# Three tokens of a head side by side on a partition for the first k and q, and the last row tile in two PSUM banks: a sparse attention with a gated FFN on one core

## The chip, the cores and the metric

The kernel runs on one core of a Trainium2 chip (trn2). The metric is the time of one execution on the device in microseconds (us). The engines are called as in the profile: PE (TensorE, matmuls and transposes), PEld (the loading of weights into PE), DVE (VectorE), ACT (ScalarE), POOL (GpSimd) and SP (SyncE, which issues most transfers).

## What is computed

For 4 batches, 8 heads, 768 tokens and 64 values a head, a query may look at the 6 best of the 24 chunks of 32 keys; a bound from each chunk's smallest and largest key decides which. The result, one row of 512 for each of 3072 tokens, goes through a root mean square norm and a gated FFN.

```python
ub = np.sum(np.maximum(q[:, :, :, None, :] * k_min[:, :, None, :, :], q[:, :, :, None, :] * k_max[:, :, None, :, :]), axis=-1)
ub = np.where(causal, ub, -1000000000.0)
top_chunks = np.argsort(ub, axis=-1)[..., -top_k:]
scores = scale * np.matmul(q, k.transpose(0, 1, 3, 2))
...
mask = sel & (pos[:, None] >= pos[None, :])
scores = np.where(mask, scores, -1000000000.0)
...
return np.matmul(attn, v).astype(np.float32)
```

```python
rms = np.sqrt(np.mean(x * x, axis=-1, keepdims=True) + 1e-06)
xn = x / rms * rms_g
g = xn @ w_gate
silu = g * (1.0 / (1.0 + np.exp(-g)))
val = xn @ w_val
return (silu * val @ w_out).astype(np.float32)
```

## The kernel before

**Work.** The 32 heads are taken as 16 pairs, four pairs a batch. For each pair `prep` (L487) loads k and q (tile names `knat`, `qnat`), turns them on PE (`turn`, L522, tiles `pk` and `pq`), copies them out of PSUM to `kt` and `qt` (`out_`, L535), takes each chunk's smallest and largest key, computes the bounds (`ub`, from pair 6 on for two pairs at once in `duo`, L778), turns these back (`up`), and picks the chunks on DVE. `scores` (L851) then does the scores (`sc`, L876), the exponentials on ACT (`pt`, L893) and the product with v (`av`, L912). When all four pairs of a batch are done, `norm` (L945) makes the normed rows and turns them (`tp` on PE for the first batch, a transposing transfer for the others) into `xT`, and `ffn` (L1025) does, for each half batch of 384 rows, 12 gate and 12 value products (`gp` L1045, `vp` L1066) and then three row tiles of 128 rows with 12 projections each (`po`, L1086), a copy out of PSUM (`osb`, `poE`) and an output transfer of 128 x 512 values (L1101).

**Loads of k and q.** `load` (L499) issues one transfer for each head of the pair (four for each tensor of pair 0, which is loaded in two halves of three row tiles). Token t of a head lies on partition t mod 128, so each partition takes one token of 64 f32 values, 256 bytes in a run, six times for each head. In the tile the two heads of a token lie side by side. `turn` transposes, for each of three row tiles, 128 partitions x 128 values (both heads) at once; three such results, 384 tokens in their order, fill one PSUM bank. From pair 3 on (`QM`, `side_q`) the natural q is also copied to `qn` and turned by a transfer; for the first three pairs the turned and cast q is used alone.

**Order.** Every piece of work is a step of a planner (`Order`, L79) with an engine, a duration, what it depends on, and the buffers it opens. `run` (L98) plays the steps through in a plan of its own: whenever an engine is free there, it takes the ready step with the lowest rank whose buffers are free. A step's rank is the sum of its place (`TIMES`: a for a pair's preparation, l for its loads, s for its scores, n and f for norm and FFN, and a pace for each step within these) and of its kind (`RANK`). The steps are then written out in the plan's order, and each engine of the chip works through its own list in that order, waiting where data is not there yet.

**Fillers.** 88 steps called `busy` (L346) multiply zeros: 48 (`BUSY`) of 512 columns (rank 1000, 1001 and so on), ready from the start, and 40 (`LATER`) of 256 columns, ready after the third pair's last scores (L920 to L923). Their ranks are above those of the other PE steps in the first batch, so that the plan puts them where PE has nothing else; all of them are in PE's list somewhere. They keep PE working while it would wait.

Of the kernel before, what the change touches and what calls it, by code (L numbers as in the profile page):

```python
# [8 lines left out]
FP32 = mybir.dt.float32  # L9
# [18 lines left out]
        av=439.71, dif=-349.0, eps=-276.35, exp=56.9, kC=119.11, kE=221.89, kT=-479.5,  # L28
        kload=-91.99, kmn=-561.73, kmx=-221.73, max=-117.69, qC=120.39, qE=644.67, qN=97.14,
        qT=303.27, qX=110.23, qload=17.43, relu=-156.64, root=392.56, sc=392.96, sel=176.91,  # L30
        selC=388.0, selT=-168.59, sq=-325.5, tp=-47.15, tpE=460.17, ub=-387.44, ubE=-1000.64,
        ubm=-238.37, up=-379.03, vload=-360.06, xb=-167.37, xs=293.02,
    ),
    dict(
        av=-243.01, dif=-122.81, eps=-968.41, exp=80.0, gate=-57.45, hh=-33.27, kC=474.21,
        kE=54.78, kT=-28.02, kload=327.35, kmn=571.37, kmx=673.95, mask=-6.85, max=351.72,
        out=-338.93, po=268.25, poE=188.61, qE=-4.14, qN=444.8, qT=271.57, qX=-691.62,
        qload=314.07, relu=202.91, root=-1348.37, sc=-186.72, sel=354.08, sq=285.76, tanh=579.3,
        tg=-259.04, ub=-101.04, ubE=-390.25, ubm=307.49, up=-117.99, val=-52.48, vload=103.56,
        xT=119.23, xb=-299.83, xs=-84.52,  # L40
# [161 lines left out]
def kernel(  # L202
# [11 lines left out]
    nc = tc.nc  # L214
# [17 lines left out]
    HW = NT * P + D  # L232
    NPAIRS = B * NP
# [253 lines left out]
    def prep(c, i0, nb, at, lr):  # L487
# [8 lines left out]
        for w, src in (("k", k), ("q", q)):  # L496
            nat[w], big[w] = Buf("nat"), Buf("qt")

            def load(e, w=w, src=src, r0=0, rn=nb):  # L499
                if nat[w].tile is None:  # L500
                    tile_of(nat[w], [P, NT, 2, D], FP32, w + "nat")
                t = nat[w].tile
                for hl in range(2):
                    eng = nc.scalar if p == 0 and hl else nc.sync
                    eng.dma_start(out=t[:, r0:r0 + rn, hl, :],  # L505
                                  in_=src[b, h0 + hl, (i0 + r0) * P:(i0 + r0 + rn) * P].rearrange(
                                      "(t p) d -> p t d", p=P))

            if p == 0:
                ld = [add(w + "load", "SP", 0.2, -200 + 2 * (w == "q") + r0 / 3,  # L510
                          lambda e, load=load, r0=r0: load(e, r0=r0, rn=3), opens=[nat[w]],
                          load=3 * P * 550) for r0 in range(0, nb, 3)]
            else:
                ld = [add(w + "load", "SP", 1.4, rank(lr, b, w + "load"), load, opens=[nat[w]],
                          load=n * 550)] * 2
# [3 lines left out]
            for j0 in range(0, nb, 3):  # L519
                bank = Buf("ps", "prep")  # L520

                def turn(e, w=w, j0=j0, bank=bank):  # L522
                    t = tile_of(bank, [P, 3 * P], FP32, "p" + w)
                    for j in range(3):
# [4 lines left out]
                tr = add(w + "T", "PE", 0.33, rank(at, b, w + "T", j0, "step"), turn, [ld[j0 // 3], c_id],  # L529
# [495 lines left out]
    def ffn(b, c, at, pace):  # L1025
# [52 lines left out]
        for th in range(3):  # L1078
            po, ob = Buf("ps", "po"), Buf("ob")
            prev = None  # L1080
            for part in range(3):
                def proj(e, th=th, part=part, po=po):
                    if part == 0:
                        tile_of(po, [P, DM], FP32, "po")
                    for ht in range(part * 4, part * 4 + 4):
                        nc.tensor.matmul(po.tile[:], hhs[ht].tile[:, th * P:(th + 1) * P],  # L1086
                                         wo[:, ht, :], start=(ht == 0), stop=(ht == NHT - 1))
# [3 lines left out]
                prev = add("po", "PE", 0.867, place("po"), proj,  # L1091
# [3 lines left out]
            def out_(e, po=po, ob=ob):  # L1095
                t = tile_of(ob, [P, DM], FP32, "osb")
                evict(e, t[:], po.tile[:], 0.5)

            o = add("poE", "", {"ACT": act(512), "DVE": dve(512)}, place("poE"), out_, [prev], opens=[ob], uses=[po])
            r0 = b * S + c * W + th * P  # L1100
            add("out", "SP", 0.55, place("out"), lambda e, r0=r0, ob=ob: nc.sync.dma_start(  # L1101
                out=out[r0:r0 + P, :], in_=ob.tile[:]), [o], uses=[ob])
# [56 lines left out]
```

## Time and profile before

| | |
|---|---|
| median of 3 runs | 315.96 us (315.95 to 316.0) |
| profiled execution | 315.79 us |
| its span, first to last instruction | 314.0 us |
| granted PE clock, mean | 1.000 |
| `pk` transposes, all pairs (L525) | 96 |
| `pq` transposes, all pairs (L525) | 96 |
| fillers (L346) | 88, of them 48 of 512 columns and 40 of 256 |
| projections (L1086) | 288, of 512 columns |
| output transfers (L1101) | 24, 256 KB each, the last issued at 310.9 us |
| DMA packets under 512 B | 106224 of 113301 |

In the profile each line of the chain in order of time has a start, a duration and an engine with its tile and line; "x6" is the number of instructions that it holds. A wait for several things is put down to the one that came last. The ends of matmuls are modelled: in lists of instructions by group a matmul of 128 columns has some 0.27 us, from its start to its last result, while the next one starts far earlier; the durations in the chain are from start to start and are the ones to add up.

### The profile page before, as it was taken

How to read it: one execution, taken by the hardware profiler on the slowest of the kernel's cores; microseconds unless marked ns; L12 is line 12 of the kernel's file. 1: busy time of each engine (PE TensorE's matmuls, PEld its weight loads, DVE VectorE, ACT ScalarE, POOL GpSimd, SP SyncE). 2: the span in 40 equal slices, each digit the busy share in tenths (PEclk: the TensorE clock that was granted, in tenths of full speed). 3: DMA queues.
4: the chain of work that ended last, by engine and by line, in shares of the span. 5: the costliest groups of instructions: out<-in, count | busy, mean ns of one | idle time of the engine just before them, and what ended most of it. 6: DMA issues, size and time to landing. Idle time of an engine off the chain costs nothing.

```text
span 314.0 us, 7640 instructions
## 1 busy us (share of the span) xinstructions
PE 308.6 (98%) x2844; PEld 196.1 (62%) x2844; DVE 230.7 (73%) x654; ACT 194.4 (62%) x420; POOL 100.7 (32%) x157
## 2 busy tenths in 40 slices
PE   7999999999999999999999999999999999999995
PEld 4567877666566775666667565656666645655542
DVE  7699986888988487967986799879464663873530
ACT  5589987863475987478579654344988823333321
POOL 8666534342353564045357300001522220000000
PEclk9999999999999999999999999999999999999999
DMA  8999989989989898979934640002341045001102
GB/s 171 210 190 178 145 108 207 198 114 143 196 86 199 126 179 152 201 164 222 158 79 61 93 102 0 2 2 52 84 94 59 20 118 150 3 0 65 38 22 111
DMA packets 113301, 35.36 MB, mean 113 GB/s; under 512 B 106224, under 2 KB 110064, under 8 KB 113264
## 3 DMA queue, kind: packets, MB, share of 16 engines
q1 hardware_dynamic: 83152, 26.62, 40.9%
q0 software_dynamic: 28512, 7.87, 25.6%
q10 hardware_dynamic: 1600, 0.39, 0.6%
q8 instruction: 22, 0.36, 0.5%
q14 instruction: 15, 0.12, 0.1%
HBM read 28.57 MB, written 6.29 MB: 111 GB/s over the span
## 4 chain that ended last, share of the span: by engine, by line
PE 97%; DMA 1%; ACTq 0%; ACT 0%; issue 0%
PE gp L1045 20%; PE vp L1066 20%; PE po L1086 20%; PE sc L876 12%; PE av L912 7%; PE busy L346 4%; PE pq L525 4%; PE pk L525 3%; PE ub L789 2%; PE ub L731 2%; DMA qnat<-in_q_dram 1%; PE up L811 1%; PE sc L882 1%; PE up L755 1%; PE tp L1011 0%; ACTq L505 0%
## 5 line engine op out<-in xcount | busy, mean ns | idle before, releaser
L893 ACT ACTIVATE pt<-sc 128x512 bf16<-128x512 f32 (+2 forms) x192 | 88.4, 578 | 10.1 <-PE sc L876 5.3
L1052 ACT ACTIVATE sg<-gp 128x384 bf16<-128x384 f32 x96 | 47.7, 500 | 62.7 <-PE gp L1045 60.0
L1066 PE MATMUL vp<-xT,wv 128*128 128x384 bf16 x384 | 77.0, 326 | 0.0
L1045 PE MATMUL gp<-xT,wg 128*128 128x384 bf16 x384 | 76.2, 326 | 0.0
L1086 PE MATMUL po<-wo,hh 128*128 128x512 bf16 x288 | 69.3, 379 | 0.0
L1058 DVE SCALAR_TENSOR_TENSOR tg<-sg,gp 128x384 bf16<-128x384 bf16 x96 | 52.2, 548 | 21.7 <-ACT sg L1052 19.5
L1074 DVE TENSOR_TENSOR hh<-vp,tg 128x384 bf16<-128x384 f32 x96 | 51.8, 551 | 11.1 <-PE vp L1066 7.3
L1045 PEld LDWEIGHTS <-wg 128*128 128x128 bf16 x384 | 36.8, 98 | 24.5 <-issue 1.0
L1066 PEld LDWEIGHTS <-wv 128*128 128x128 bf16 x384 | 36.9, 98 | 24.1
L876 PE MATMUL sc<-qs,ke 128*128 128x128 bf16 (+5 forms) x420 | 51.4, 251 | 0.0
L1086 PEld LDWEIGHTS <-hh 128*128 128x128 bf16 x288 | 27.6, 98 | 27.5
L301 POOL CAST ke<-kt 64x768 bf16<-64x768 f32 x31 | 26.4, 852 | 36.9 <-ACT kt L297 17.0
L876 PEld LDWEIGHTS <-ke 128*128 128x128 bf16 (+1 forms) x420 | 30.3, 97 | 11.3 <-issue 1.6
L899 POOL TENSOR_SCALAR_AFFINE_SELECT pt<-pt 128x512 bf16<-128x512 bf16 (+1 forms) x48 | 24.4, 527 | 37.6 <-ACT pt L893 37.4
L912 PEld LDWEIGHTS <-pt 128*128 128x128 bf16 x672 | 28.8, 98 | 7.7 <-POOL ke L301 0.6
L912 PE MATMUL av<-vx,pt 128*128 128x65 bf16 x672 | 32.6, 193 | 0.0
L299 ACT ACTIVATE osb<-po 128x512 f32<-128x512 f32 x19 | 11.4, 602 | 21.4 <-PE po L1086 21.4
L346 PE MATMUL busy<-zeros 128*128 128x512 bf16 (+1 forms) x88 | 20.1, 349 | 1.3 <-DVE zeros L341 1.3
L933 DVE TENSOR_TENSOR xb<-av,rden 128x384 bf16<-128x384 f32 (+1 forms) x34 | 18.1, 534 | 1.2
L989 DVE SCALAR_TENSOR_TENSOR xs<-xb,ri,gains 128x512 bf16<-128x512 bf16 x24 | 16.9, 746 | 2.7 <-DMA xT<-xs 2.1
L301 POOL CAST qn<-qnat 128x768 bf16<-128x768 f32 x10 | 8.2, 821 | 31.9 <-DMA qs<-qn 30.7
L481 POOL DMA_DIRECT2D vx<-in_v_dram x16 | 16.8, 1052 | 4.0 <-PE av L912 2.6
(87 smaller groups left out, 303.1 us busy)
## 6 DMA issues: line engine op xcount, KB each, us to landing
out_dram<-osb SPq DMA_DIRECT2D x24, 256.0 KB, 2.2
knat<-in_k_dram SPq DMA_DIRECT2D x30, 192.0 KB, 4.3
qnat<-in_q_dram SPq DMA_DIRECT2D x30, 192.0 KB, 4.8
vx<-in_v_dram POOLq DMA_DIRECT2D x16, 192.0 KB, 4.7
wg<-in_moe_w_gate_dram POOLq DMA_DIRECT2D x2, 768.0 KB, 8.6
wv<-in_moe_w_val_dram POOLq DMA_DIRECT2D x2, 768.0 KB, 7.8
wo<-in_moe_w_out_dram POOLq DMA_DIRECT2D x2, 768.0 KB, 9.9
qs<-qn SPq DMA_TRANSPOSE x26, 3.3
```

What stands on the lines that cost most here:

```text
L301: engine[e].tensor_copy(out_, in_)
L346: nc.tensor.matmul(t[:, 0:n], zeros[:, 0:P], zeros[:, 0:n], start=True, stop=True)
L876: nc.tensor.matmul(t[:, x:x + m, :].rearrange("p a b -> p (a b)"), ke[kk, kb * P:(kb + 1) * P], qs[kk, q0 * P:(q0 + m) * P], start=not tri ...
L893: nc.scalar.activation(out=t[:, 0:nn, :], in_=sc.tile[:, 0:nn, :], func=ACT.Exp, scale=SCALE)
L899: nc.gpsimd.affine_select(out=pt.tile[:, 0:nd, :], in_=pt.tile[:, 0:nd, :], compare_op=ALU.is_ge, fill=0.0, base=0, pattern=[[0, nd], [1, ...
L912: nc.tensor.matmul(av.tile[:, qi - i0, :], pt.tile[:, x, :], VX[c.v.slot][:, hl * NT + kb, :], start=(begin and m == 0), stop=(left[0] == ...
L1045: nc.tensor.matmul(t[:], wg[:, g, hs], XT[b].tile[:, g, cols], start=(g == 0), stop=(g == NP - 1))
L1052: nc.scalar.activation(out=t[:], in_=gp.tile[:], func=ACT.Tanh, scale=0.5)
L1058: nc.vector.scalar_tensor_tensor(out=t[:], in0=sg.tile[:], scalar=1.0, in1=gp.tile[:], op0=ALU.add, op1=ALU.mult)
L1066: nc.tensor.matmul(t[:], wv[:, g, hs], XT[b].tile[:, g, cols], start=(g == 0), stop=(g == NP - 1))
L1074: nc.vector.tensor_tensor(out=t[:], in0=vp.tile[:], in1=tg.tile[:], op=ALU.mult)
L1086: nc.tensor.matmul(po.tile[:], hhs[ht].tile[:, th * P:(th + 1) * P], wo[:, ht, :], start=(ht == 0), stop=(ht == NHT - 1))
```

## The change

For the first three pairs (`WIDE`), each partition takes three tokens that follow each other, so that a run in memory is 3 x 64 values, 768 bytes; the tile holds the two heads apart: [128, 2 heads, 2 halves, 3 tokens, 64]. Partition p then holds tokens 3p, 3p+1 and 3p+2 of each half of 384. `turn` transposes each of the three token places by itself and writes the columns to every third word of the bank, so the bank holds the 384 tokens in their order as before. Since the two heads no longer lie side by side, one transpose takes 128 values that end with the second head's token place (its lower 64 result rows are right, the upper 64 are those of something else), and a second one of 64 values overwrites the upper 64 rows with the first head. The planner's costs for these steps follow: 0.66 instead of 0.33 for a turn, 330 instead of 550 for a row of a load.

In the last half batch, the third row tile's projection is made in two parts of 256 columns, each with a PSUM tile, a copy and an output transfer of its own.

All values of the planner's tables `RANK` and `TIMES` are replaced; `BUSY`, `LATER`, the slots and the limits are not. Of the tables only some lines are shown here.

```diff
@@ -25,38 +25,38 @@
 
 RANK = (
     dict(
-        av=439.71, dif=-349.0, eps=-276.35, exp=56.9, kC=119.11, kE=221.89, kT=-479.5,
...
+        av=531.52, dif=-599.99, eps=-382.83, exp=-161.96, kC=439.01, kE=22.86, kT=-498.41,
...
 TIMES = {
...
-    133.0, "a7": 70.59, "a8": 128.02, "a9": 121.26, "f0.0": 33.65, "f0.1": 8.37, "f1.0": -84.59,
-    "f1.1": 458.33, "f2.0": 528.25, "f2.1": 57.29, "f3.0": 75.85, "f3.1": 711.78, "ke": 138.67,
...
-    "n3.1": 574.2, "pace0": -0.69, "pace1": 11.25, "pacef0.0": 0.39, "pacef0.1": 15.72,
-    "pacef1.0": 11.97, "pacef1.1": 14.19, "pacef2.0": 25.48, "pacef2.1": 21.31, "pacef3.0":
-    -30.15, "pacef3.1": 4.73, "pacen": -9.51, "qn0": -62.11, "s0.0": -763.02, "s1.0": -94.31,
...
+    "a7": 109.83, "a8": 49.55, "a9": 39.08, "f0.0": -72.94, "f0.1": -64.96, "f1.0": -71.83,
+    "f1.1": -48.5, "f2.0": -120.42, "f2.1": -73.36, "f3.0": -52.32, "f3.1": -51.07, "ke":
...
+    "n3.1": -636.32, "pace0": 0.45, "pace1": 10.85, "pacef0.0": 3.71, "pacef0.1": 19.42,
+    "pacef1.0": 16.78, "pacef1.1": 6.12, "pacef2.0": 20.36, "pacef2.1": 14.59, "pacef3.0":
+    -41.53, "pacef3.1": 9.68, "pacen": -19.58, "qn0": -12.11, "s0.0": -499.62, "s1.0": 233.49,
...
@@ -230,6 +230,7 @@
     DUO = 6
     KSIDE, QM = 16, 3
     HW = NT * P + D
+    WIDE = dict(k=3, q=3)
     NPAIRS = B * NP
 
     SLOTS = dict(ps=8, nat=7, kb=0, qn=2, vext=4, set=3, ku=4, selq=2, qt=7, ubs=1, ubd=1, small=8, ubm=3,
@@ -496,7 +497,19 @@
         for w, src in (("k", k), ("q", q)):
             nat[w], big[w] = Buf("nat"), Buf("qt")
 
-            def load(e, w=w, src=src, r0=0, rn=nb):
+            wide = p < WIDE[w]
+
+            def load(e, w=w, src=src, r0=0, rn=nb, wide=wide):
+                if wide:
+                    if nat[w].tile is None:
+                        tile_of(nat[w], [P, 2, 2, 3, D], FP32, w + "nat")
+                    t, j, jn = nat[w].tile, r0 // 3, rn // 3
+                    for hl in range(2):
+                        eng = nc.scalar if p == 0 and hl else nc.sync
+                        eng.dma_start(out=t[:, hl, j:j + jn],
+                                      in_=src[b, h0 + hl, r0 * P:(r0 + rn) * P].rearrange(
+                                          "(j p t) d -> p j t d", j=jn, t=3))
+                    return
                 if nat[w].tile is None:
                     tile_of(nat[w], [P, NT, 2, D], FP32, w + "nat")
                 t = nat[w].tile
@@ -509,24 +522,32 @@
             if p == 0:
                 ld = [add(w + "load", "SP", 0.2, -200 + 2 * (w == "q") + r0 / 3,
                           lambda e, load=load, r0=r0: load(e, r0=r0, rn=3), opens=[nat[w]],
-                          load=3 * P * 550) for r0 in range(0, nb, 3)]
+                          load=3 * P * (330 if wide else 550)) for r0 in range(0, nb, 3)]
             else:
                 ld = [add(w + "load", "SP", 1.4, rank(lr, b, w + "load"), load, opens=[nat[w]],
-                          load=n * 550)] * 2
+                          load=n * (330 if wide else 550))] * 2
             ready[w] = ld
 
             evs = []
             for j0 in range(0, nb, 3):
                 bank = Buf("ps", "prep")
 
-                def turn(e, w=w, j0=j0, bank=bank):
+                def turn(e, w=w, j0=j0, bank=bank, wide=wide):
                     t = tile_of(bank, [P, 3 * P], FP32, "p" + w)
+                    if wide:
+                        flat = nat[w].tile[:].rearrange("p h j t d -> p (h j t d)")
+                        for j in range(3):
+                            cols_ = t[:].rearrange("q (p j) -> q j p", j=3)
+                            x = (j0 + j) * D
+                            nc.tensor.transpose(cols_[:, j], flat[:, NT * D + x - D:NT * D + x + D], ident_f[:])
+                            nc.tensor.transpose(cols_[0:D, j], flat[:, x:x + D], ident_f[:])
+                        return
                     for j in range(3):
                         nc.tensor.transpose(
                             t[:, j * P:(j + 1) * P],
                             nat[w].tile[:, j0 + j].rearrange("p h d -> p (h d)"), ident_f[:])
 
-                tr = add(w + "T", "PE", 0.33, rank(at, b, w + "T", j0, "step"), turn, [ld[j0 // 3], c_id],
+                tr = add(w + "T", "PE", 0.66 if wide else 0.33, rank(at, b, w + "T", j0, "step"), turn, [ld[j0 // 3], c_id],
                          opens=[bank], uses=[nat[w]])
                 if w == "k" and side_k:
                     kbanks.append((j0, bank, tr))
@@ -1075,31 +1096,33 @@
 
             hh_done.append(add("hh", "DVE", dve(W), place("hh"), mul, [a, d], opens=[hh], uses=[vp, tg]))
             hhs.append(hh)
-        for th in range(3):
+        last = b == B - 1 and c == 1
+        for th, c0, cn in [(th, c0, DM >> (last and th == 2)) for th in range(3)
+                           for c0 in ((0, DM // 2) if last and th == 2 else (0,))]:
             po, ob = Buf("ps", "po"), Buf("ob")
             prev = None
             for part in range(3):
-                def proj(e, th=th, part=part, po=po):
+                def proj(e, th=th, part=part, po=po, c0=c0, cn=cn):
                     if part == 0:
-                        tile_of(po, [P, DM], FP32, "po")
+                        tile_of(po, [P, cn], FP32, "po")
                     for ht in range(part * 4, part * 4 + 4):
                         nc.tensor.matmul(po.tile[:], hhs[ht].tile[:, th * P:(th + 1) * P],
-                                         wo[:, ht, :], start=(ht == 0), stop=(ht == NHT - 1))
+                                         wo[:, ht, c0:c0 + cn], start=(ht == 0), stop=(ht == NHT - 1))
 
                 hs = range(part * 4, part * 4 + 4)
                 step()
-                prev = add("po", "PE", 0.867, place("po"), proj,
+                prev = add("po", "PE", 0.867 if cn == DM else 0.44, place("po"), proj,
                            [prev] + [hh_done[i] for i in hs] + c_wo, opens=[po],
                            uses=[hhs[i] for i in hs])
 
-            def out_(e, po=po, ob=ob):
-                t = tile_of(ob, [P, DM], FP32, "osb")
+            def out_(e, po=po, ob=ob, cn=cn):
+                t = tile_of(ob, [P, cn], FP32, "osb")
                 evict(e, t[:], po.tile[:], 0.5)
 
-            o = add("poE", "", {"ACT": act(512), "DVE": dve(512)}, place("poE"), out_, [prev], opens=[ob], uses=[po])
+            o = add("poE", "", {"ACT": act(cn), "DVE": dve(cn)}, place("poE"), out_, [prev], opens=[ob], uses=[po])
             r0 = b * S + c * W + th * P
-            add("out", "SP", 0.55, place("out"), lambda e, r0=r0, ob=ob: nc.sync.dma_start(
-                out=out[r0:r0 + P, :], in_=ob.tile[:]), [o], uses=[ob])
+            add("out", "SP", 0.55, place("out"), lambda e, r0=r0, ob=ob, c0=c0, cn=cn: nc.sync.dma_start(
+                out=out[r0:r0 + P, c0:c0 + cn], in_=ob.tile[:]), [o], uses=[ob])
 
 
     pairs = []
```

More of the change, by code (lines that the diff above doesn't have):

```diff
@@ L27 @@
     dict(
-        av=439.71, dif=-349.0, eps=-276.35, exp=56.9, kC=119.11, kE=221.89, kT=-479.5,
[L29 to L32, printed above, removed]
+        av=531.52, dif=-599.99, eps=-382.83, exp=-161.96, kC=439.01, kE=22.86, kT=-498.41,
+        kload=-19.25, kmn=-447.62, kmx=-228.82, max=-248.4, qC=107.35, qE=746.95, qN=298.65,
+        qT=519.06, qX=-151.47, qload=-24.59, relu=-460.62, root=129.7, sc=365.93, sel=257.61,
+        selC=551.79, selT=-231.19, sq=-154.83, tp=271.95, tpE=468.58, ub=-335.26, ubE=-1193.04,
+        ubm=-112.18, up=-462.73, vload=-472.52, xb=-225.95, xs=320.45,
     ),
     dict(
[L35 to L40, printed above, removed]
+        av=-271.42, dif=-54.99, eps=-1240.6, exp=295.6, gate=-64.89, hh=-195.53, kC=482.39,
+        kE=246.36, kT=30.32, kload=287.64, kmn=567.66, kmx=613.76, mask=-124.96, max=535.32,
+        out=-272.89, po=479.34, poE=192.97, qE=-47.6, qN=259.48, qT=361.69, qX=-804.45,
+        qload=318.6, relu=556.6, root=-1442.33, sc=-179.66, sel=175.66, sq=318.54, tanh=758.86,
+        tg=-469.07, ub=-181.01, ubE=-458.81, ubm=369.37, up=-51.94, val=-28.21, vload=312.74,
+        xT=51.55, xb=-496.58, xs=-229.89,
     ),
```

20 rows, old and new, of the table TIMES are left out of this document.

## The prediction

> **What bounds the kernel now.** I read the page first, then the list of waits on TensorE (PE), then the busy time by stretches, then the chain of waits in order of time.
>
> ```profile
> span 314.0 us, 7640 instructions
> PE 308.6 (98%) x2844; PEld 196.1 (62%) x2844; DVE 230.7 (73%) x654; ACT 194.4 (62%) x420; POOL 100.7 (32%) x157
> PE 97%; DMA 1%; ACTq 0%; ACT 0%; issue 0%
> ```
>
> The chain that ended last lies on PE for 97% of the span. The ends of matmuls are modelled, so a busy PE alone proves little; the list of everything PE waited for over the whole span settles it:
>
> ```profile
> engine line waited for: us in total, times, longest us
> PE busy L346 <- DVE zeros L341: 1.3, 1, 1.3
> PE pq L525 <- DMA qnat<-in_q_dram: 0.3, 1, 0.3
> ```
>
> There are two waits: 1.3 us until the first instruction, and 0.3 us for q of the first pair. Everything else is PE working through its list back to back. Next, by stretch (columns: busy us and count of PE, PEld, DVE, ACT, POOL; granted clock, DMA share, GB/s):
>
> ```profile
> 0.00:6.00 6.00, 4.41 (x16) 2.06 (x17) 4.33 (x13) 2.16 (x4) 5.19 (x19) 1.00 0.76 158
> 6.00:18.00 12.00, 12.00 (x115) 7.18 (x114) 8.62 (x28) 7.71 (x13) 8.04 (x12) 1.00 0.99 213
> 18.00:38.00 20.00, 20.00 (x276) 15.32 (x275) 19.49 (x70) 19.64 (x44) 12.14 (x15) 1.00 1.32 169
> 38.00:54.00 16.00, 15.97 (x230) 12.39 (x228) 13.26 (x46) 13.64 (x33) 6.12 (x9) 1.00 1.04 150
> 54.00:310.00 256.00, 256.00 (x2216) 159.16 (x2214) 184.97 (x500) 150.60 (x328) 69.24 (x104) 1.00 0.59 100
> ```
>
> and the same stretches for the tile "busy" alone, the fillers of L346 that compute nothing (busy us and count of PE):
>
> ```profile
> 0.00:6.00 6.00, 3.59 (x8) 1.00 0.76 158
> 6.00:18.00 12.00, 6.48 (x27) 1.00 0.99 213
> 18.00:38.00 20.00, 2.00 (x7) 1.00 1.32 169
> 38.00:54.00 16.00, 8.04 (x46) 1.00 1.04 150
> 54.00:310.00 256.00, 0.00 (x0) 1.00 0.59 100
> ```
>
> So there are two regimes. Up to 54 us PE is dense only because 88 fillers stand in its list; what really limits there is, in 6 to 18, the loading (DMA share 0.99, DVE busy 8.62 of 12, ACT 7.71), then ACT and DVE (19.64 and 19.49 of 20). From 54 on there is no filler left and PE is full with real work. The border is sharp:
>
> ```profile
> 52.89 1.08 PE busy L346 x5
> 53.97 3.90 PE gp L1045 x24
> ...
> 302.89 7.35 PE po L1086 x34
> ```
>
> ```profile
> 52.10 1.54 ACT L297 ACTIVATE xT<-tp 128x512 bf16<-128x512 bf16 x3
> ```
>
> The last five fillers end as the first gate product starts, just after ACT has copied out its input (52.10 + 1.54 = 53.64): those fillers covered a true wait, and none was left over. PE ends at 302.89 + 7.35 = 310.24; eviction and output fill the rest of the span. The profiled execution took 315.79 us, so 315.79 - 314.05 = 1.74 lie outside the span; the runs' median, 315.96, is 0.17 above it.
>
> From this follows the rule I use for the whole sum. PE has a fixed list: all real work and exactly 88 fillers, whose number the diff does not touch. It waits 0.3 us in all after its start. So its end is its start plus the sum of its list, **whatever comes earlier elsewhere**; what can still move are the length of the list, the 0.3 us, and what stands behind PE's last useful instruction.
>
> **The change part by part.**
>
> *Loads.*
>
> ```profile
> knat<-in_k_dram SPq DMA_DIRECT2D x30, 192.0 KB, 4.3
> qnat<-in_q_dram SPq DMA_DIRECT2D x30, 192.0 KB, 4.8
> ```
>
> The same number of DMA issues on the same queues (two for each tensor and pair, four for pair 0), so nothing is added to SP's or ACT's list and no step is queued behind more of them. Packets become a third in number and three times as long. The bytes are 2 x 192 KB for each of six tensors, 2.36 MB; at the 213 GB/s of the stretch from 6 to 18 this is 11.1 us of loading.
>
> ```profile
> 311.00:312.00 1.00, 0.00 (x0) 0.00 (x0) 0.00 (x0) 0.00 (x0) 0.00 (x0) 1.00 0.81 305
> ```
>
> At the 305 GB/s that outputs (2 KB runs) reach in this stretch near the end it would be 7.7 us. So up to 3.4 us less loading, of which the chain to the first gate product gains between nothing and 3.4, since ACT and DVE are full from 18 to 38. By the rule this does not shorten PE's list; it only turns covered waits into fillers that are no longer needed where they stood. What it can give at once is the wait for q: -0.34 at most, 0 at least; I take -0.34, because that wait is a load's.
>
> *Turning.* A bank of three row tiles takes six transposes instead of three: for each tile a full one (whose lower half is right) and one of 64 columns that overwrites the upper half. Three pairs, k and q, six tiles each: 36 more on PE.
>
> ```profile
> 17.30 0.34 PE st L702 x6
> 17.63 0.34 PE up L755 x4
> 17.97 0.66 PE pq L525 x6
> ```
>
> Six now take 0.66, 0.110 each. The moving operand of the narrow ones is the same identity of 128 columns, so 36 x 0.110 = +3.96. No narrow f32 transpose is in the trace. From below, 0.057 (the bf16 turn of 128 columns, 0.34 / 6) would give +2.1; from above I allow each narrow one twice the price, +7.9, if the change of width between neighbours hinders the loading of weights. I take 0.110: it is the row of the same operation and type.
>
> The results now go to every third word of the bank. Nothing in the trace writes so; `up` (L755) writes runs of 32 words and takes 0.34 / 4 / 96 = 0.89 ns a column, `pq` without any gap 0.110 / 128 = 0.86. The projection writes 512 f32 columns in 7.35 / 34 = 0.216, 0.42 ns a column, so the write side can go twice as fast as a transpose needs; halved, it would still keep up. I take 0 for it, and for the upper bound that all 72 transposes double: 72 x 0.110 = +7.9 on top of the 3.96. The evictions read and write what they did.
>
> The Trainium skill has two rules against this part. "PSUM — Partial Sum Buffer", Specifications, says that any non-contiguous access slows matmuls significantly. "TensorEngine Tiling (Array Packing)", Restrictions, says that column tiling disables the f32 transpose mode, and a transpose of 64 columns could count as such. By these the sum would be some 4 to 8 us higher; by the rows above it is not, and no run here has shown either yet. They stand behind the second rival.
>
> *The cover of these transposes.* The last of the six tensors is the third q, the row at 17.97 above, so they lie among the 8 + 27 fillers of the first 18 us, where PE has time: as work they delay nothing there. But the fillers whose place they take are not removed. The planner gives PE a filler (rank 1000 and more) whenever no real step is ready in its plan, so the 3.96 us of fillers go to the next moment at which its plan sees PE idle. That is the "late next": if such a moment comes after 54 us, PE in truth has none to spare there (256.00 of 256.00), and the filler costs its whole length.
>
> *Last row tile.* 12 projections of 512 columns become 24 of 256.
>
> ```profile
> 49.61 0.87 PE busy L346 x8
> ...
> 310.25 0.03 ACTq L299
> 310.27 0.04 issue
> 310.32 0.60 ACT osb L299
> ```
>
> ```profile
> 10.77 0.38 ACT L297 ACTIVATE ubs<-ub 96x256 f32<-96x256 f32 x1 [0.71 <-PE ub L731]
> ```
>
> ```profile
> 310.08 1.20 SPq L1101 DMA_DIRECT2D out_dram<-osb  x2
> ```
>
> PE: 24 x 0.87 / 8 - 12 x 0.216 = 2.61 - 2.59 = +0.02. The last eviction falls from 0.60 to about 0.38, -0.22. One more eviction and one more issue on SP come earlier, under the second half's 12 x 0.109 = 1.3 us of matmuls, which covers an eviction (0.38) and an issue (1.20 for two, less than 0.6). The last output is 128 KB instead of 256; at 305 GB/s that is -0.43, and 0 if its landing is all latency; I take -0.3. Together -0.5, with -0.2 to -0.65 as bounds.
>
> *Order.* All ranks and start times are replaced, so nearly every step may stand elsewhere, DMA issues too. PE waits 0.3 us after its start now, so a new order can hardly win there and may lose; I take 0, bounds 0 to +3.6 (fourth case).
>
> Sum: 315.79 + 3.96 + 0.02 - 0.34 - 0.5 = **318.9** in the profile's terms, 319.1 against the median; I say 318.9, some 0.9% slower. Its own range, from the idle and tail terms and from fillers of up to 1.5 us that still find a free place, is 317.2 to 319.6.
>
> **Rivals.**
>
> *Displaced fillers go behind the last projection (not slower).* If the plan is dense from the first gate product on, as the trace is, no idle moment takes the spare fillers, and they stand at the end of PE's list, during the eviction and output that follow now from 310.24 to 314.05, 3.8 us. Place: after the last matmul of L1086; price: nothing while they fit. PE's list still has to be finished: 310.24 + 3.96 + 0.02 - 0.34 = 313.9, and the useful work ends earlier by what the loads gain. The span is then about PE's own end, 313.9, the time 315.6; if the quicker loads also take out short stalls that the model of matmul ends hides up to 6 us (PE is busy 4.41 of 6.00, 0.33 beyond the 1.26 before its start, and a filler takes 3.59 / 8 = 0.45 there against 1.08 / 5 = 0.22 at 52.89), 314.6 to 315.3. It decides from the point at which about 3.3 us of fillers stand behind. For it: not one filler and not one wait in 256 us. Against it: any idle instant of the plan, however short, draws in a whole filler, and ACT and DVE are busy 59% and 72% of that stretch.
>
> *The change doesn't do cheaply what it says.* Strided writes or narrow transposes are dearer: with one of the two bounds above, 318.9 + 4.0 = 322.9; with both, 326 to 331, which I hold for remote. For it: no row shows either. Against it: the rates above.
>
> *The new order opens holes.* The new times of the FFN steps (f0.0 to f3.1) all lie near -50 to -120, where they were spread from -85 to 712, so FFN goes ahead of the attention of later batches, and the last batch's attention could stand without FFN to cover it. In 18 to 38 the attention alone left PE 2.00 idle of 20, 10%; a batch's 36 us (18 to 54) at that rate gives up to +3.6, 322.5. Against it: the steep pace values spread the FFN steps again.
>
> **How the numbers follow.** Forecast 39%, fillers behind the end 37%, dearer transposes 12%, holes 12%. A measurement of this kernel can tell about 0.2%, 0.63 us, from no change: below 315.33 is faster, above 316.59 slower. The first rival lies across the lower line: 23 of its 37 below it, where the stalls of the first 6 us shrink, and 14 within. The other three are slower: 39 + 12 + 12 = 63. For 8 in 10 I leave out the lowest 5% (below 314.8) and most of the dear transposes with the deepest holes, some 13%: 314.8 to 322.2.
>
> **What would show it.** In the profile after: PE's instructions rise by 36 + 12; `pq` and `pk` of the first three pairs take about 1.32 for 12 in the chain (2.6 if the second rival holds); the fillers' count stays 88, and their place by stretch decides between forecast (some after 54, before the last projection) and first rival (a run of them after it). The last osb eviction is near 0.38. The list of waits on PE shows whether the order opened holes. The forecast is wrong if PE's last projection ends at 310.5 or earlier.

## The result and the profile after

| | before | after |
|---|---|---|
| time, median (lowest to highest), us | 315.95 (315.8 to 316.0) | 320.65 (319.61 to 321.33) |
| profiled execution, us | 315.79 | 319.61 |
| ratio with 95% interval | | 1.0147 [1.0119, 1.0174] |

The changed kernel is 1.5% slower, +4.7 us in the medians. Its runs spread over 1.7 us where those of before spread over 0.2; the profiled one is its fastest. What follows reads that execution, which is 3.8 us longer than the profiled one of before.

The page, span and PE line:

```profile
span 317.9 us, 7732 instructions
PE 311.6 (98%) x2870; PEld 201.8 (63%) x2892; DVE 228.4 (72%) x653; ACT 197.5 (62%) x422; POOL 100.0 (31%) x157
```

Weight loads rose by 48, from 2844 to 2892: the 36 transposes and 12 half projections are there (22 matmul records are missing). But the list of PE's waits is another one:

```profile
PE pk L542 <- DMA knat<-in_k_dram: 1.8, 2, 1.2
PE busy L347 <- DVE zeros L342: 1.3, 1, 1.3
PE po L1109 <- issue: 0.5, 3, 0.2
PE tp L1032 <- ACT kt L298: 0.4, 1, 0.4
PE pq L542 <- DMA qnat<-in_q_dram: 0.3, 1, 0.3
```

Before, 0.3 us after the start; now 3.0, of which 2.1 for loads of k and q. By stretch (columns as before):

```profile
0.00:6.00 6.00, 4.19 (x14) 2.35 (x15) 3.37 (x11) 2.17 (x3) 5.19 (x19) 1.00 0.65 185
6.00:18.00 12.00, 10.39 (x109) 7.25 (x108) 10.28 (x31) 6.96 (x11) 9.31 (x13) 1.00 1.22 214
54.00:310.00 256.00, 254.31 (x2216) 159.74 (x2234) 183.59 (x513) 152.76 (x331) 69.48 (x104) 1.00 0.59 97
```

PE is dense no longer from 6 to 18 (10.39 of 12, before 12.00). The fillers alone, in stretches cut at the first gate product (60.39) and at the end of the last projection (314.03); a filler that lies across a border counts on both sides:

```profile
0.00:18.00 18.00, 4.96 (x15) 1.00 1.03 204
18.00:54.00 36.00, 5.86 (x26) 1.00 1.13 170
54.00:60.39 6.39, 1.80 (x12) 1.00 1.14 186
60.39:314.03 253.64, 3.37 (x20) 1.00 0.57 95
314.03:318.00 3.97, 2.76 (x14) 1.00 0.21 71
```

In the first 18 us 15 are left of 35, and some 33 now stand behind the first gate product: about 18 before the last projection's end and 15 behind it. The chain of waits, from three of its windows:

```profile
5.14 5.90 DMA knat<-in_k_dram
11.04 0.14 issue
11.17 0.30 PE pk L542
11.47 0.11 PE pk L543
...
12.68 1.01 PE ub L752 x24
...
60.39 5.20 PE gp L1066 x32
...
308.82 5.21 PE po L1109 x36
314.03 0.43 PE busy L347 x3
```

Two readings. A narrow transpose (L543) takes 0.11, as a full one does. And the chain of the first 12 us is no longer PE but a load: k of pair 1 lands at 11.04, with nothing in PE's list ahead of its transposes to fill the time. The difference in length can be laid out on three marks of the two chains: the first gate product starts at 60.39 where it was 53.97, **+6.42**; from there to the end of the last projection it is 253.64 where it was 310.24 - 53.97 = 256.27, **-2.63**; from there to the end of the span 3.87 where it was 3.81, **+0.06**. The marks say where the time lies, not yet what cost it: fillers take 12.62 us ahead of the first gate product (4.96 + 5.86 + 1.80) where they took 20.11 (3.59 + 6.48 + 2.00 + 8.04), so the new order does more of the real work there, and the stretch behind it is shorter only because of that, with 18 fillers in it that were not there before. The divided last tile gave nothing on the marks. Why is in the timeline of the end (start, duration, what, in brackets the idle time of the engine before it), and in the last line of the chain:

```profile
310.58 0.60 ACT L300 ACTIVATE osb<-po 128x512 f32<-128x512 f32 x1 [5.78 <-PE po L1109]
311.21 4.28 SPq L1124 DMA_DIRECT2D out_dram<-osb  x4
311.45 0.60 ACT L300 ACTIVATE osb<-po 128x512 f32<-128x512 f32 x1 [0.27 <-PE po L1109]
313.63 0.38 ACT L300 ACTIVATE osb<-po 128x256 f32<-128x256 f32 x1 [1.59 <-PE po L1109]
314.75 0.38 ACT L300 ACTIVATE osb<-po 128x256 f32<-128x256 f32 x1 [0.73 <-PE busy L347]
```

```profile
314.52 2.32 PE busy L347 x11
```

The last copy takes 0.38, as forecast, but begins 0.72 after the last projection has ended (314.03). The releaser named, a filler, is none of its inputs. The three half-batch rows give four copies now, and there are three osb buffers (`ob=3`): the fourth copy takes the buffer of the first, whose output was issued at 311.21 and landed at 314.64, 0.11 before the copy began. A second thing holds the end as long: the fillers behind the last projection run until 314.52 + 2.32 = 316.84, and the last output lands at 316.86. The order with the old layout, below, shows that the fillers alone would have been enough.

One thing more is in PE's timeline. Its durations are modelled and overlap, so read the distance of the starts:

```profile
6.07 0.42 PE L543 MATMUL pk<-ident_f,knat 128*64 128x128 f32 x1
6.28 0.41 PE L542 MATMUL pk<-ident_f,knat 128*128 128x128 f32 x1
...
6.64 0.27 PE L542 MATMUL pq<-ident_f,qnat 128*128 128x128 f32 x1
6.75 0.27 PE L543 MATMUL pq<-ident_f,qnat 128*64 128x128 f32 x1
```

Until about 6.5 us the transposes of pair 0 start every 0.21, from there on every 0.11. PE begins at half pace, though the granted clock stands at 1.00 throughout; in the kernel before it is at full pace from about 4.7 us on.

### The profile page after: what moved, and what is told of

Read it like the earlier page. It is cut to its first block, busy times and chain, and to the rows that moved or that the text cites. A ratio compares the mean times of both kernels' runs of the same rounds, so it can differ in the third digit from the quotient of the medians.

```text
span 317.9 us, 7732 instructions
## 1 busy us (share of the span) xinstructions
PE 311.6 (98%) x2870; PEld 201.8 (63%) x2892; DVE 228.4 (72%) x653; ACT 197.5 (62%) x422; POOL 100.0 (31%) x157
## 4 chain that ended last, share of the span: by engine, by line
PE 95%; DMA 3%; issue 1%; ACT 1%; ACTq 0%
PE vp L1087 20%; PE gp L1066 20%; PE po L1109 19%; PE sc L897 12%; PE av L933 6%; PE busy L347 4%; PE pq L546 3%; PE pk L546 3%; PE ub L810 2%; PE ub L752 2%; DMA knat<-in_k_dram 2%; DMA qnat<-in_q_dram 1%; PE up L832 1%; PE sc L903 1%; PE up L776 1%
## 5 line engine op out<-in xcount | busy, mean ns | idle before, releaser
L914 ACT ACTIVATE pt<-sc 128x512 bf16<-128x512 f32 (+1 forms) x192 | 88.6, 578 | 6.8 <-PE sc L897 5.9
L1087 PE MATMUL vp<-xT,wv 128*128 128x384 bf16 x384 | 75.2, 326 | 0.0
L1066 PE MATMUL gp<-xT,wg 128*128 128x384 bf16 x384 | 73.5, 326 | 0.0
L1109 PE MATMUL po<-wo,hh 128*128 128x512 bf16 (+1 forms) x283 | 64.4, 370 | 1.2 <-issue 0.5
L897 PE MATMUL sc<-qs,ke 128*128 128x128 bf16 (+5 forms) x418 | 54.3, 250 | 0.1
L933 PEld LDWEIGHTS <-pt 128*128 128x128 bf16 x672 | 32.3, 98 | 8.4 <-issue 0.8
L933 PE MATMUL av<-vx,pt 128*128 128x65 bf16 x672 | 37.3, 193 | 0.1
L300 ACT ACTIVATE osb<-po 128x512 f32<-128x512 f32 (+1 forms) x22 | 12.7, 577 | 29.1 <-PE po L1109 28.2
L302 POOL CAST ke<-kt 64x768 bf16<-64x768 f32 x30 | 24.7, 828 | 19.1 <-PE sc L897 10.8
L347 PE MATMUL busy<-zeros 128*128 128x512 bf16 (+1 forms) x85 | 18.8, 344 | 1.4 <-DVE zeros L342 1.3
```

What stands on the lines that cost most here:

```text
L302: engine[e].tensor_copy(out_, in_)
L347: nc.tensor.matmul(t[:, 0:n], zeros[:, 0:P], zeros[:, 0:n], start=True, stop=True)
L897: nc.tensor.matmul(t[:, x:x + m, :].rearrange("p a b -> p (a b)"), ke[kk, kb * P:(kb + 1) * P], qs[kk, q0 * P:(q0 + m) * P], start=not tri ...
L914: nc.scalar.activation(out=t[:, 0:nn, :], in_=sc.tile[:, 0:nn, :], func=ACT.Exp, scale=SCALE)
L933: nc.tensor.matmul(av.tile[:, qi - i0, :], pt.tile[:, x, :], VX[c.v.slot][:, hl * NT + kb, :], start=(begin and m == 0), stop=(left[0] == ...
L1066: nc.tensor.matmul(t[:], wg[:, g, hs], XT[b].tile[:, g, cols], start=(g == 0), stop=(g == NP - 1))
```

## The experiments

Two families: the *new order* (the changed kernel's tables) with something taken out, and the *old order* (the tables of before) with one part of the change put in. Each ratio is against runs of the kernel before on the same chip, whose medians were 316.01 to 316.13.

### The 36 narrow transposes taken out of the new order

```diff
-                            nc.tensor.transpose(cols_[0:D, j], flat[:, x:x + D], ident_f[:])
```

> The changed kernel with the 36 narrow transposes left out (the upper 64 rows of k and q of three pairs are then wrong values); every list keeps its order. Theory (PE's list is what ends last, but PE now waits for loads in the first 11 us, and what lies before such a wait is covered): the 12 of pair 0 stand before the wait for pair 1's k and give nothing, the other 24 give 24 x 0.110 = 2.6 us, so 318.0 against 320.65 for the changed kernel; up to 3.96 less (316.7) if the waits do not grow. Rival (fillers and waits cover them all, and the new order is what costs): 320.2 or more.

Measured: 321.09 (320.04 to 321.73), ratio 1.0155 [1.013, 1.018]: nothing gained. The list of waits, two lines of PE's timeline and one of the chain:

```profile
PE pq L542 <- DMA qnat<-in_q_dram: 3.0, 2, 2.1
PE pk L542 <- DMA knat<-in_k_dram: 1.2, 2, 0.9
```

```profile
3.84 1.51 PE L542 MATMUL pk<-ident_f,knat 128*128 128x128 f32 x6 [0.27 <-DMA knat<-in_k_dram]
9.82 1.51 PE L542 MATMUL pq<-ident_f,qnat 128*128 128x128 f32 x6 [2.14 <-DMA qnat<-in_q_dram]
```

```profile
12.26 1.51 PE pk L542 x6
```

Two things take the place of the 36 transposes. PE waits 4.2 us for loads, where the changed kernel waits 2.1. And it stays at half pace until about 16.7 us: six full transposes take 1.51, as much as the twelve of the changed kernel from 11.17 to 12.68, which start 0.11 apart. So in this order leaving the transposes out saves nothing. That is not to say that they are free there: whether the half pace lasted because they were gone, or by chance in this execution, one trace does not show.

### The fillers behind the first gate product taken out of the new order

```diff
+    seen = False
     for s in done:
+        seen = seen or s.name == "gate"
+        if s.name == "busy" and seen:
+            continue
         s.emit(s.eng)
```

> The changed kernel without the 33 fillers that stand behind the first gate product in PE's list: 18 between 73 and 79 us (14 of 256 and 4 of 512 columns, 2.39 us) and 15 behind the last projection. Theory (displaced fillers cost their length where PE is full): 2.4 us less for the 18, and those behind the end give nothing more, since the last output lands at the same moment as the last of them ends: about 318.2. Rival (the 18 cover true waits, as the fillers before the first gate product do): 320.3 or more, and PE shows waits of some 2 us between 73 and 79.

Measured: 318.39 (318.1 to 318.74), ratio 1.0076 [1.0059, 1.0092], -2.3: the expected number, but the trace does not bear out the reason. The two profiled executions differ by 1.5 only, on the marks +0.47, -1.31 and -0.6. From the first gate product (60.86) to the end of the last projection (305.38 + 7.81 = 313.19) it is 252.33 instead of 253.64, so 18 fillers of 2.4 us (14 of 256 columns at 0.108 and 4 of 512 at 0.216, by the rows of before) save 1.3. In the chain stands what some of them covered:

```profile
78.04 0.48 DVE hh L1095
78.52 0.04 issue
78.56 0.81 PE vp L1087 x4
```

DVE, 9.81 us busy of the 10 from 70 to 80 in both traces, is late with `hh`, and PE waits for it. The -0.6 is the tail: the span ends 3.2 after the last projection instead of 3.9. The 15 fillers behind it are gone, and so is the wait for the osb buffer (the last copy starts at 313.26, 0.07 after the last projection), since the outputs of 256 KB landed in some 2.0 us there, and the first of the changed kernel's in 3.4 (311.21 to 314.64). The order with the old layout, below, shows that these fillers hold the end by themselves, so the expectation that leaving them out gives nothing more does not hold.

### Wide loads and six transposes in the old order

`RANK` and `TIMES` are those of before, and so is the plan's price of a turn (0.33) and of a load:

```diff
-                          load=3 * P * (330 if wide else 550)) for r0 in range(0, nb, 3)]
+                          load=3 * P * 550) for r0 in range(0, nb, 3)]
...
-        last = b == B - 1 and c == 1
+        last = False
```

> The kernel before, with its own tables, plan costs and order of every list, and its undivided last row tile; only the loads of the first three pairs are wide and their turns take six transposes. Theory (PE's list is dense from 6 us on, so each added transpose counts): 315.95 + 3.96 - up to 0.3 = 319.6 to 319.9. Rival A (the wide loads bring the chain to the first gate product forward and the transposes lie under waits): 316.5 or less. Rival B (the new order is what costs, not the layout): about 316.

Measured: 319.32 (318.89 to 319.65), ratio 1.0101 [1.0086, 1.0116], +3.3. The chain and the waits:

```profile
57.48 3.90 PE gp L1066 x24
...
304.63 9.51 PE po L1109 x44
```

```profile
PE gp L1066 <- DMA xT<-xs: 0.2, 1, 0.2
```

Behind the start this is the only wait: PE is dense as before and waits for no load of k or q; the first gate product starts 3.5 later (57.48 against 53.97). In a list that is full of fillers, 36 transposes are 36 transposes more: close to the 3.96.

### The divided last tile in the old order, and with one output tile for both halves

The first takes the tables, loads and three transposes of before, and keeps only the two banks. The second also puts both halves into one osb tile:

```diff
+        shared = Buf("ob")
...
-            po, ob = Buf("ps", "po"), Buf("ob")
+            po, ob = Buf("ps", "po"), shared if cn < DM else Buf("ob")
...
-                t = tile_of(ob, [P, cn], FP32, "osb")
-                evict(e, t[:], po.tile[:], 0.5)
+                if ob.tile is None:
+                    tile_of(ob, [P, DM], FP32, "osb")
+                evict(e, ob.tile[:, c0:c0 + cn], po.tile[:], 0.5)
```

> The kernel before, with its own tables and layout; only the last row tile is projected, copied out and stored in two halves. Theory: the fourth copy of the last half batch has to wait for one of three osb buffers, whose output is still on its way, so the gain is small: 0 to -0.3, 315.65 to 315.95. Rival (the tail shortens as predicted, by an eviction of 0.38 instead of 0.60 and half a transfer): 315.45.

> The kernel before with its tables and layout and the last row tile in two halves, as in the fourth run, but both halves copied into one osb tile, so that no fourth buffer is needed. Theory (the halves gain the shorter copy and the smaller transfer, and no buffer is waited for in this order anyway): the same as the fourth run, 315.5. Rival (the buffer still costs there): 315.2 or less.

Measured: 315.51 (315.38 to 315.79), ratio 0.9985 [0.9976, 0.9995], -0.5; and 315.24 (314.98 to 315.48), ratio 0.9969 [0.9958, 0.9981], -0.9. So the divided tile is worth what the prediction gave it, more than I expected after seeing the tail above. That sharing the buffer adds to it is not shown: in the first of the two traces, too, the last copy starts 0.07 after the last projection (310.58 against 310.51), the tails are equally long (3.2), and the second is ahead by 0.45 already at the first gate product, where PE came to full pace earlier (by 4.6 us, against after 6.3). The end of the second:

```profile
310.13 0.38 ACT L300 ACTIVATE osb<-po 128x256 f32<-128x256 f32 x1 [1.15 <-PE po L1110]
```

The last copy starts 0.07 after the last projection (310.06), and span's end follows 3.2 after it, against 3.8 before.

### The new order with the old loads and three transposes

```diff
             wide = p < WIDE[w]
+            laid = False
...
-            def load(e, w=w, src=src, r0=0, rn=nb, wide=wide):
+            def load(e, w=w, src=src, r0=0, rn=nb, wide=laid):
...
-                def turn(e, w=w, j0=j0, bank=bank, wide=wide):
+                def turn(e, w=w, j0=j0, bank=bank, wide=laid):
```

> The changed kernel with its own lists (order, places of the fillers, divided last tile), but k and q of the first three pairs loaded as before, 256 bytes in a run, and turned by three transposes a bank. Theory (the new order was planned for loads at 0.6 of the price and transposes at twice the price, so its fillers stand late and PE waits for loads in the first 12 us; the 36 transposes lie under these waits): between the run without narrow transposes and the changed kernel less what earlier landing of pair 1's k gives (landing 5.2 us after issue before, 5.8 after): 319.5 to 321. Rival (the wide loads and their late landing cause the waits): 317.5 or less, and the waits of PE for k and q fall under 0.5 us.

Measured: 320.57 (319.58 to 323.46), ratio 1.0169 [1.0129, 1.0209]. Without the layout the new order is just as slow. It waits for the narrow loads as for the wide ones, and PE stays at half pace until about 14 us (six transposes in 1.51):

```profile
PE pk L547 <- DMA knat<-in_k_dram: 1.3, 2, 1.1
PE pq L547 <- DMA qnat<-in_q_dram: 1.0, 1, 1.0
```

```profile
5.72 4.91 DMA knat<-in_k_dram
...
10.77 1.51 PE pk L547 x6
```

```profile
314.16 0.39 ACT osb L300
314.55 0.01 issue
314.56 2.32 PE busy L347 x11
```

The end of this trace takes the two holds of the changed kernel's tail apart. The first output lands 2.0 us after its issue here, so no buffer is waited for: the last copy starts at 314.16, 0.08 after the last projection (314.08), and the last output lands at 316.27. The span still ends 3.8 after the last projection, at 317.9, because the fillers run until 316.88. As long as they stand there, the divided tile has nothing to shorten.

### Wide loads in the old order, 18 fillers fewer

```diff
+        if s.name == "busy":
+            fill += 1
+            if 8 < fill <= 26:
+                continue
```

> The third run (the order before, wide loads, six transposes a bank) without 18 of its 48 long fillers, the 9th to the 26th, which stand between 7 and 17 us: 18 x 0.216 = 3.9 us of PE's list, as much as the 36 transposes add. Theory (PE's list sets the end, but pair 1's k, landing at about 11.1, becomes a wait of some 1.5 us): 319.3 - 3.9 + 1.5 = 316.9. If nothing waits: 315.4. Rival (the fillers cover true waits throughout): 319 or more, with 3 to 4 us of waits on PE before 18 us.

Measured: 317.4 (317.14 to 317.93), ratio 1.004 [1.0027, 1.0054]. The 18 fillers (3.9 us) gave 1.9. The waits that took their place are not loads:

```profile
PE ub L752 <- DVE qt L302: 1.4, 1, 1.4
```

### The gains transfer moved behind the loads, in both orders

The transfer of the norm's gains (256 KB) is issued among the first loads of k and q and is needed only by `norm`. Here it is written out behind the twelfth of those loads:

```diff
+    at = [i for i, s in enumerate(done) if s.name in ("kload", "qload")][11]
+    g = [s for s in done if s.name == "gains"]
+    done = [s for s in done[:at + 1] if s.name != "gains"] + g + [s for s in done[at + 1:] if s.name != "gains"]
```

> The changed kernel with one transfer issued later: the 256 KB of gains, which SP issues at 4.1 us ahead of pair 1's loads, go out behind the twelfth k or q load; nothing else is moved. Theory (pair 1's k lands late because it stands behind the gains on the DMA engines): its landing comes from 11.0 to about 9.5, PE's waits for k and q fall from 2.1 to under 0.8 us, and the time by 1 to 2: 318.7 to 319.7. Rival (the wide loads themselves land late, or the chain behind them on DVE and ACT sets the first 60 us): 320.2 or more.

> The kernel before with the last row tile in halves that share one osb tile (315.24 so far), and the gains transfer behind the twelfth load of k and q. Theory (PE's list is fixed and dense in this order, PE waits 0.3 us for a load after its start): loads land earlier, the time stays within 314.9 to 315.3. Rival (the first 6 us hold stalls behind late loads that the list of waits does not show): 314.5 or less.

Measured: in the new order 318.71 (318.46 to 318.80; a fourth run took 464.55 and is left out), ratio 1.0077 [1.0062, 1.0093], -1.9 (the profiled executions differ by 1.0). In the old order, beside the shared output tile, 315.08 (314.51 to 315.57), ratio 0.997 [0.9959, 0.998], against 315.24 without the move: nothing. The new order's list of waits on PE now reads:

```profile
PE pq L542 <- DMA qnat<-in_q_dram: 0.4, 1, 0.4
PE pk L542 <- DMA knat<-in_k_dram: 0.3, 1, 0.3
```

k of pair 1 lands at 9.25 instead of 11.04, and the waits for loads fall from 2.1 to 0.7. The same edit is worth 1.9 where PE waits for loads and nothing where fillers stand in that place. This run also shows that the osb buffer's wait changes from run to run; the last projection ends at 312.29, 1.74 earlier than in the changed kernel, but the last copy begins 1.35 later, and its output, landing at 315.74, comes after the last filler:

```profile
313.64 0.39 ACT osb L300
```

### Everything together

Three runs. The new order with the gains moved, the late fillers out and the output tile shared; the old order with the gains moved, the tile shared and the 9th to 14th filler out; and the old order with the wide loads, the gains moved, the tile shared and 18 fillers out. The edits are those shown.

> The changed kernel with three costs taken out at once: the gains transfer issued behind the twelfth load of k and q, the 33 fillers behind the first gate product left out, and both halves of the last row tile copied into one osb tile. Theory (the excess of the new order is these separate terms): 320.65 - 1.9 - 2.3 - 0.3 = 316.1, about the kernel before. Rival (the terms share one cause, for instance the fillers behind the first gate product cover what the late loads leave open): no better than 317, and the list of waits on PE shows more than the 2 us that it shows with the gains transfer moved alone.

> As the run before, and the 9th to 14th filler left out (six of some 0.24 us, 1.4 us). Theory (earlier loads set covers free, which is worth time only when the fillers go too): 315.1 - 1.4 = 313.7, waits on PE still under 0.6. Rival (the fillers cover copies and bounds by ACT and DVE, not loads): 314.6 to 315.2, and PE waits for kt, qt or ub in their place.

> Wide loads and the six transposes in the order of before, with 18 fillers left out (317.4 so far), the last row tile in halves sharing one osb tile, and the gains transfer behind the twelfth load of k and q. Theory (with 18 fillers gone PE waits for DVE and ACT, not for k): -0.9 for the tail, 0 to -0.5 for the loads: 316.0 to 316.5, so the layout costs even then. Rival (loads still limit the first 18 us): 314.6 to 315.2, as -1.9 for the loads comes on top, and the layout is worth having.

Measured:

| | us, median (lowest to highest) | ratio with 95% interval |
|---|---|---|
| new order, all three | 315.9 (315.71 to 316.67) | 1.0003 [0.9994, 1.0013] |
| old order, narrow, six fillers out | 314.3 (313.85 to 314.51) | 0.9943 [0.9926, 0.996] |
| old order, wide, 18 fillers out | 316.88 (316.38 to 317.81) | 1.0033 [1.002, 1.0046] |

The first is the theory's number: with the loads set free, the 33 late fillers out and the tile shared, the new order's excess of 4.7 is gone, with all 36 transposes still in. Three things speak against reading it as three clean terms. The -2.3 of the late fillers already holds the tail, so the sum of the theory counts it twice. Its profiled run, its slowest, still shows 1.9 us of waits for loads. And the kernel that it ties with has 33 fillers more to work through, so the new order is not shown to be as good as the old one.

The second is the fastest kernel of all, 0.57% under the one before. It fell between theory and rival: -0.8 where six fillers make up some 1.4. PE's list ends at 309.58, 0.66 earlier than before, with one short new wait (`ub` on ACT's `rt`, 0.2). So some of those fillers did cover something; 0.2 of it is in the list, the rest I could not place.

The third missed its expectation by 0.4 on the slow side. It waits for `qt` as the kernel of the section above, 1.4 us, loads set free or not. With these numbers of fillers the layout still loses, 316.88 against 314.3; other numbers were not run.

## Why the prediction was right, and what in its sum was not

The forecast, 318.9 and slower, held, and 320.65 lies in its range. That its sum came so near is partly luck, since two errors in it cancel. On the profiled executions PE's last projection ends 3.79 later (314.03 against 310.24). The sum up to there has 3.96 + 0.02 - 0.34. The list of waits has +2.7 (3.0 against 0.3) where the sum took 0 for the order and -0.34 for the load; and 15 fillers, 2.81 us (314.03 to 316.84), went behind the last projection where the sum let all of them stay ahead. 3.96 + 0.02 + 2.7 - 2.81 is 3.87. This leaves out that PE stayed at half pace some 2 us longer, so it closes only roughly. The experiments add that the terms are not independent: with the transposes out, waits and half pace take their place.

- **The rule (PE's list is fixed and dense)** held for the old order: with the wide loads there PE waits for no load, and moving the gains transfer gives nothing. It failed for the changed kernel, in the step "PE waits 0.3 us after its start now, so a new order can hardly win there and may lose; I take 0". This is the step that went wrong. The new order with the old layout takes 320.57, as much as the changed kernel, so the order alone is enough for the loss. The place was wrong too: the fourth case looked for holes in the last batch's attention, and they are in the first 12 us, where 5 fillers are left of those that covered the loads.
- **36 narrow transposes, +3.96.** Price right (0.11 each), and true as a cost in the old order (+3.3 for layout and transposes together). In the new order taking them out gains nothing, since PE then waits 2.1 longer and keeps half pace until about 16.7 us.
- **Dearer transposes.** False. `L543` writes 64 rows to every third word and takes 0.11 like `L542`. The two rules of the Trainium skill that stood behind this rival, "PSUM — Partial Sum Buffer", Specifications (non-contiguous access slows matmuls), and "TensorEngine Tiling (Array Packing)", Restrictions (no f32 transpose mode under column tiling), don't show here: stride and width change nothing in the trace.
- **The loads, -0.34.** Wrong sign: waits for k and q rose from 0.3 to 2.1. k of pair 1 landed at 11.04, and with the narrow loads in the same order at 10.63; in the old order at 11.14 and 10.10 in two traces with wide loads, at 9.63 to 9.93 in three with narrow ones. The fewer, longer packets did not make it land earlier.
- **The displaced fillers.** Forecast and first rival each got about half: 18 came before the last projection, 15 behind it. Behind it they cost no more than the tail of before (3.9 against 3.8), as the first rival said, but they took the divided tile's gain. The 18 cost 1.3 us of their 2.4, since DVE's `hh` was late behind them; "the filler costs its whole length" was too much for that place.
- **The tail, -0.5.** Right in size in the old order (-0.5). In the new one the gain was eaten (+0.06 on the tail), by two things that the step did not name: the fourth copy waited for one of three osb buffers, and the fillers behind the last projection ran until the last output had landed. Either is enough: the fillers without the wait in the order with the old layout, the wait beyond the fillers in the run with the gains moved. The shared tile's -0.9 is not shown to be more than the -0.5.

What was not tried: the new order without the 15 last fillers alone, and the new order planned with the old load price of 550. That the planner put its fillers late because it believed in loads at 330 fits the order that it made, and is argued, not shown.

## What to carry to other kernels

When an order is replaced along with a layout, price the two apart: a dense engine is dense because of the order, and what hides a load (here fillers) is itself a place in it. A term of a sum that is right in one order can save nothing when it is taken out of another, so ask of each what will set the end in the order that will run. And when one copy becomes two, count the buffers that it goes to, and look what else still runs behind the last result: a gain there shows only when everything that ends late ends earlier.

## What was not expected of the hardware

- PE begins every traced execution at half pace (transposes start 0.21 apart) and comes to full pace (0.11) once, while the granted clock reads 1.00. The moment differs: between 4.4 and 7.4 us in twelve of the traces, about 14 in the new order with the old layout, about 16.7 without the narrow transposes. The fillers of 0.45 against 0.22 that the prediction saw in the first 6 us are this. A wait after that moment did not bring half pace back: without the late fillers PE waits 2.0 us and goes on at full pace:

```profile
11.53 0.30 PE L542 MATMUL pk<-ident_f,knat 128*128 128x128 f32 x1 [1.97 <-DMA knat<-in_k_dram]
11.67 0.27 PE L543 MATMUL pk<-ident_f,knat 128*64 128x128 f32 x1
11.78 0.27 PE L542 MATMUL pk<-ident_f,knat 128*128 128x128 f32 x1
```

  Before that moment, the two late traces have PE waiting 0.8 and 1.0 us at about 6 us and again later, while in the other twelve no wait between PE's start and the moment is longer than 0.6. That fits waits putting it off, but two traces do not show it, and how much of the runs' spread comes from it stays open.
- A transfer that nobody needs yet delays those beside it: with the 256 KB of gains moved away, k of pair 1 landed 1.8 us earlier (9.25 against 11.04), 0.2 of it because it was issued earlier, and in the old order with wide loads 1.9 earlier (8.20 against 10.10), 0.9 of it by the issue. Why packets three times as long did not land earlier stays open.
